# A fused attention and softplus MLP kernel: attention walked by batch in two windows, its instructions listed by a small planner, and a 512-token tail

## Chip, cores and metric

One core of a Trainium2 chip runs the whole program. The metric is the device time of one execution in microseconds, as the median of the runs taken. Five engines share the work: TensorE (PE, matmuls; PEld is its weight load), VectorE (DVE), ScalarE (ACT), GpSimd (POOL) and SyncE (SP, which here only issues DMAs).

## The reference

```python
# B, H, S, D = 4, 8, 576, 64; d_ff = 2048
scores = scale * q @ k.T          # causal mask, softmax over keys
local  = softmax(scores) @ v
q_p    = phi(q)                   # elu(q) + 1
mem    = (q_p @ M_prev) / (q_p @ z_prev + 1e-6)
out    = g * mem + (1 - g) * local          # g = sigmoid(beta), one per head
x      = out as [B * S, H * D]              # 2304 tokens x 512
y      = softplus(x @ w_in) @ w_out         # w_in, w_out arrive as 64-bit floats
```

Float32 accuracy is kept by splitting an operand into a rounded part and a remainder ("hi" and "lo") and adding three products (hi·hi, hi·lo, lo·hi). A product of the MLP is therefore three matmuls per 128-row slice.

## The kernel before

**Attention.** A unit is one batch and one pair of heads; 16 units run in the order batch, pair. Each has five chunks of query rows (four of 128, one of 64 rows for both heads). A chunk c goes: scores on PE (L292, mask L295), row maximum on DVE (L309), exponent on ACT (L312, written as a softplus with a shifted bias), reciprocal on DVE (L332, L333), the hi part on POOL (L337) and the lo part on DVE (L339), a DMA transpose from SP (L342), and two chunks later the product with the values on PE (L380, PSUM tile `xp`), where the memory term was put first (L369). ACT copies `xp` into the resident array `x` (L387). `prep_items` (L229) does a unit's value scaling and memory product; `loads` (L217) brings q, k and v for a unit.

**MLP.** The 16 f-tiles (128 of the 2048 columns) are handled in groups of 5, 5 and 6, since weights are decoded from 64-bit words on the chip (`split64`, L120: four DVE operations, two on POOL, one on ACT for each of two pieces of an f-tile). The tokens are cut into 8 blocks of 288 (`CAP`). For a block and an f-tile (an f-step here) there are 12 matmuls into `hp` (`emit_h`), a softplus and a split into `g` (`emit_g`), and 12 matmuls out. Group 0 of a block can run inside attention as a "fill" (`push_fill`, L180), once its whole batch has its `x`; the partial result goes to DRAM (`part`). The rest is phase 2 (L485 on): the blocks of group 0 that were not filled, then groups 1 and 2 over all 8 blocks. Each step splits its `x` block anew (`split_x`, L175; ACT and DVE in phase 2, DVE and POOL in a fill) and adds into `ps`, a resident sum; the last group stores each block. The output product of an f-step is issued three f-steps after its input product (`LAG`).

**What sets the order.** The framework's scheduler orders each engine's instructions by priority and a modelled time; every engine then runs its list strictly in that order. The number of fills in a slot is set by `credit` (L473), and weight pieces by `wcred` (L478).

Of the kernel before, what the change touches and what calls it, by code (L numbers as in the profile page):

```python
# [15 lines left out]
U32 = mybir.dt.uint32  # L16
# [8 lines left out]
TINY = 2.0 ** -15  # L25
# [4 lines left out]
GRPS = [5, 5, 6]  # L30
GA = GRPS[0]


class Unit:
    chunks = [0, 1, 2, 3, 4]

    def __init__(self, b, p):
        self.b, self.p = b, p
        self.pt = {}
        self.xp = None  # L40
# [3 lines left out]
def attn_softplus_moe(  # L44
# [13 lines left out]
    WIDE = w_in.dtype == I64  # L58

# [3 lines left out]

# [13 lines left out]
    wt = {}  # L77

    wa = ctx.enter_context(tc.tile_pool(name="wa", bufs=1, reuse_waits="tile"))
    moe1 = ctx.enter_context(tc.tile_pool(name="moe1", bufs=1))  # L80
    CAP = S // 2
    NFILL = 6
    nb = NT // CAP
    done = set()

    V, A, P, SY = nc.vector, nc.scalar, nc.gpsimd, nc.sync
# [11 lines left out]


    def load_w(pool, f, stage, sb, tag=None):  # L100
        t = pool.tile([128, 2, 2, 512], F32R, tag=tag or f"w{f}", name=f"w{f}")
        wt[f] = t

        def piece(i):
            src = w_out[f * 128:(f + 1) * 128, :] if i else w_in[f]
            hi, lo = t[:, i, 0, :], t[:, i, 1, :]
            if not WIDE:
                s = stage.tile([128, 512], F32, tag="ws", name="ws", bufs=sb)
                SY.dma_start(out=s, in_=src)
                cast(A, hi, s)  # L110
                sub(P, lo, s, hi)
            else:
                s = stage.tile([128, 1024], F32, tag="ws", name="ws", bufs=sb)
                tu = stage.tile([128, 512], F32, tag="wu", name="wu", bufs=sb)
                SY.dma_start(out=s.bitcast(I32), in_=src.bitcast(I32))
                split64(s, tu, hi, lo)

        return [lambda: piece(0), lambda: piece(1)]

    def split64(s, tu, hi, lo):  # L120

        sw = s.rearrange("p (e t) -> p e t", t=2)
        si = s.bitcast(I32).rearrange("p (e t) -> p e t", t=2)
        ti = tu.bitcast(I32)
        V.tensor_scalar(out=ti, in0=si[:, :, 1], scalar1=1, scalar2=1, op0=ALU.logical_shift_left,  # L125
                        op1=ALU.logical_shift_right)
        P.tensor_scalar(out=tu, in0=tu, scalar1=3.0e38, scalar2=TINY, op0=ALU.min, op1=ALU.max)  # L127
        V.tensor_scalar(out=ti, in0=ti, scalar1=3, scalar2=0x3FFFFFFF, op0=ALU.logical_shift_left,  # L128
                        op1=ALU.bitwise_and)
        V.scalar_tensor_tensor(out=ti, in0=si[:, :, 1], scalar=-0x40000000, in1=ti, op0=ALU.bitwise_and,  # L130
                               op1=ALU.bitwise_or)
        V.scalar_tensor_tensor(out=ti, in0=si[:, :, 0], scalar=29, in1=ti, op0=ALU.logical_shift_right,  # L132
                               op1=ALU.bitwise_or)
        cast(A, hi, tu)
        sub(P, lo, tu, hi)


    def mm3(out, pairs, start, stop):
        n = len(pairs)
        for i, (l, r) in enumerate(pairs):  # L140
            nc.tensor.matmul(out, lhsT=l, rhs=r, start=start and i == 0, stop=stop and i == n - 1)  # L141

    hcnt = []
    PB_ = {'h': 2, 'xp': 1, 'sm': 1}

    def emit_h(pool, f, xh, n, cap):
        w = wt[f]
        tags = ["h"] if not hcnt else ["h", "h", "xp", "sm"]
        tag = tags[hcnt[0] % len(tags)] if hcnt else "h"
        hp = ps_r.tile([128, 512], F32, tag=tag, name="hp", bufs=PB_[tag])  # L150
        if hcnt:
            hcnt[0] += 1
        pairs = []
        for kd in range(4):
            wh, wl = w[:, 0, 0, kd * 128:(kd + 1) * 128], w[:, 0, 1, kd * 128:(kd + 1) * 128]
            pairs += [(wh, xh[:, 0, kd, :n]), (wh, xh[:, 1, kd, :n]), (wl, xh[:, 0, kd, :n])]
        mm3(hp[:, :n], pairs, True, True)
        return hp

    def emit_g(pool, hp, n, cap, gb):  # L160
        l = pool.tile([128, cap], F32, tag="l", name="l", bufs=3)[:, :n]
        g = pool.tile([128, 2, cap], F32R, tag="g", name="g", bufs=gb)
        A.activation(out=l, in_=hp[:, :n], func=AF.Softplus)  # L163
        cast(A, g[:, 0, :n], l)
        sub(V if hcnt else P, g[:, 1, :n], l, g[:, 0, :n])
        return g

    def out_pairs(f, g, dm, n):
        w = wt[f]
        wh, wl = w[:, 1, 0, dm * 128:(dm + 1) * 128], w[:, 1, 1, dm * 128:(dm + 1) * 128]  # L170
        return [(wh, g[:, 0, :n]), (wh, g[:, 1, :n]), (wl, g[:, 0, :n])]

    fill = deque()

    def split_x(pool, t0, kd, xt, ea, eb):  # L175
        src = x[:, kd, t0:t0 + CAP]
        cast(ea, xt[:, 0, kd, :], src)
        sub(eb, xt[:, 1, kd, :], src, xt[:, 0, kd, :])

    def push_fill(k):  # L180
        st = {}
        t0 = k * CAP

        def xs(kd):
            if kd == 0:
                done.add(k)
                st["x"] = moe1.tile([128, 2, 4, CAP], F32R, tag="xhl", name="xhl", bufs=1)
            split_x(moe1, t0, kd, st["x"], V, P)

        def h(f):  # L190
            hp = emit_h(moe1, f, st["x"], CAP, CAP)
            st[f] = emit_g(moe1, hp, CAP, CAP, GA)

        def o(dm):
            op = ps_r.tile([128, 512], F32, tag="h", name="op", bufs=2)
            pairs = []
            for f in range(GA):
                pairs += out_pairs(f, st[f], dm, CAP)
            mm3(op[:, :CAP], pairs, True, True)
            pb = moe1.tile([128, CAP], F32, tag="pb", name="pb", bufs=2)  # L200
            A.copy(pb, op[:, :CAP])
            SY.dma_start(out=part[:, dm, t0:t0 + CAP], in_=pb)

        for kd in range(4):
            fill.append((0.0, kd == 0, lambda kd=kd: xs(kd)))
        for f in range(GA):
            fill.append((12 * CAP / 2400.0, False, lambda f=f: h(f)))
        for dm in range(4):
            fill.append((3 * GA * CAP / 2400.0, False, lambda dm=dm: o(dm)))


    units = [Unit(b, p) for b in range(B) for p in range(NP)]

    attn_ctx = ExitStack()
    at = attn_ctx.enter_context(tc.tile_pool(name="attn", bufs=1, side="right"))

    def loads(i):  # L217
        u = units[i]
        b, p = u.b, u.p
        u.kp = at.tile([128, S], F32, tag="kp", name="kp", bufs=2)  # L220
        u.va = at.tile([128, 640], F32, tag="va", name="va", bufs=2)
        u.mq = at.tile([128, 130 + S], F32, tag="mq", name="mq", bufs=2)
        SY.dma_start(out=u.mq, in_=nat[b, p, :, 640:770 + S])
        SY.dma_start(out=u.kp, in_=nat[b, p, :, 770 + S:])
        SY.dma_start(out=u.va, in_=nat[b, p, :, 0:640])
        u.vst = u.va.rearrange("p (c e) -> p c e", e=128)
        u.mz, u.qp = u.mq[:, 0:130], u.mq[:, 130:130 + S]

    def prep_items(i):  # L229
        u = units[i]  # L230
        p = u.p

        def v0():
            u.sc = at.tile([128, 5], F32, tag="sc", name="sc", bufs=3)
            si = u.sc.bitcast(I32)
            u.vb = at.tile([128, 2, 5, 128], F16, tag="vb", name="vb", bufs=2)
            jk = u.vb[:, 0].bitcast(BF16)
            for j, sg in enumerate((1.0, -1.0)):
                A.activation(out=jk, in_=u.vst, func=AF.Relu, scale=sg, accum_out=u.sc[:, 3 + j:4 + j])
            sp = ps_r.tile([128, 512], F32, tag="sm", name="sp", bufs=1)  # L240
            for j in range(2):
                nc.tensor.matmul(sp[:, 0:1], lhsT=mean, rhs=u.sc[:, 3 + j:4 + j], start=j == 0, stop=j == 1)
            V.tensor_scalar(out=si[:, 0:1], in0=sp.bitcast(I32)[:, 0:1], scalar1=0x7F800000, scalar2=None,
                            op0=ALU.bitwise_and)
            V.tensor_scalar(out=u.sc[:, 0:1], in0=u.sc[:, 0:1], scalar1=2.0 ** -60, scalar2=None, op0=ALU.max)
            V.tensor_scalar(out=si[:, 1:2], in0=si[:, 0:1], scalar1=-1.0, scalar2=float(261 << 23), op0=ALU.mult,
                            op1=ALU.add)
            V.tensor_scalar(out=u.sc[:, 2:3], in0=u.sc[:, 0:1], scalar1=2.0 ** -22, scalar2=None, op0=ALU.mult)
# [378 lines left out]
```

## Time and profile before

| | |
|---|---|
| median of 3 runs | 694.08 us (693.69 to 699.11) |
| profiled execution: span, first to last instruction | 695.3 us |
| mean granted TensorE clock | 0.937 of full speed |
| PE / DVE / ACT / POOL busy, share of span | 92% / 63% / 48% / 31% |
| HBM read, written | 34.89 MB, 7.08 MB |

The profile page gives no other time of that execution than its span. Busy shares are an average over a stage with attention, to about 353 us, and a stage with the MLP alone. A busy PE in the first stage isn't PE at its peak, since the ends of matmuls are modelled.

### The profile page before, as it was taken

What the parts mean: (1) busy time and instruction counts of PE and PEld (TensorE: products, weight loads), DVE (VectorE), ACT (ScalarE), POOL (GpSimd) and SP (SyncE); (2) the same over time, 40 slices, a digit from 0 to 9 for tenths busy, and PEclk for the clock granted to TensorE, in tenths of its full rate; (3) what the DMA queues carried; (4) which work ended last, traced back from release to release, by engine and by line L of the source; (5) the groups of instructions that cost most, each with busy time, mean ns of one, the idle gap of its engine ahead of it and who ended that gap; (6) DMA issues with size and microseconds to landing.
All of it is one profiled execution on the core that took longest, in us unless ns stands there. A gap on an engine that the chain in (4) does not pass through costs nothing.

```text
span 695.3 us, 12560 instructions
## 1 busy us (share of the span) xinstructions
PE 639.1 (92%) x4584; PEld 541.5 (78%) x4584; DVE 441.4 (63%) x1012; ACT 334.4 (48%) x949; POOL 219.0 (31%) x270
## 2 busy tenths in 40 slices
PE   6578976899999999997799999999999999999997
PEld 4344544667767666754689999999999999999997
DVE  4887999868776977858658799983333333323222
ACT  6554655457677556765354544353333333333321
POOL 3554565744544636324214545430000000000000
PEclk8667776899999999998899999999999999999999
DMA  4685778558676696747473333300000011110001
GB/s 151 154 195 131 156 170 180 95 112 185 126 150 136 111 171 128 160 107 131 80 225 110 122 119 102 115 31 1 1 1 1 1 35 35 35 35 25 28 29 59
DMA packets 124173, 68.47 MB, mean 98 GB/s; under 512 B 105680, under 2 KB 113872, under 8 KB 124112
## 3 DMA queue, kind: packets, MB, share of 16 engines
q1 hardware_dynamic: 124112, 67.67, 41.5%
q8 instruction: 36, 0.59, 0.4%
q14 instruction: 25, 0.20, 0.1%
HBM read 34.89 MB, written 7.08 MB: 60 GB/s over the span
## 4 chain that ended last, share of the span: by engine, by line
PE 37%; DVE 9%; DMA 3%; ACT 2%; issue 1%; POOL 1%; SPq 0%; DVEq 0%; ACTq 0%; POOLq 0%
PE acc L141 18%; PE hp L141 18%; DMA ws<-in_w_out_dram 2%; DVE wu L132 2%; DVE xhl L89 1%; DVE wu L130 1%; DVE wu L128 1%; DVE g L89 1%; DVE wu L125 1%; DVE PHL L339 1%; ACT P L312 1%; DVE ps L566 0%; DMA ws<-in_w_in_dram 0%; DMA PTB<-PHL 0%; ACT xhl L95 0%
## 5 line engine op out<-in xcount | busy, mean ns | idle before, releaser
L141 PE MATMUL hp<-xhl,w 128*128 128x288 f32 x1536 | 231.7, 300 | 5.7 <-DVE xhl L93 4.9
L141 PEld LDWEIGHTS hp<-xhl,w 128*128 128x128 f32 x1536 | 213.4, 191 | 8.0 <-DVE xhl L93 5.3
L141 PE MATMUL acc<-g,w 128*128 128x288 f32 x1296 | 188.6, 297 | 5.5 <-ACT P L312 2.9
L141 PEld LDWEIGHTS acc<-g,w 128*128 128x128 f32 x1296 | 177.8, 189 | 7.5 <-ACT P L312 3.0
L89 DVE TENSOR_TENSOR g<-l,g 128x288 fp32r<-128x288 f32 x108 | 57.9, 539 | 116.0 <-ACT g L95 116.0
L163 ACT ACTIVATE l<-hp 128x288 f32<-128x288 f32 x128 | 52.2, 411 | 139.2 <-PE hp L141 137.1
L337 POOL TENSOR_SCALAR PHL<-P,rr 128x128 f16<-128x128 f32 (+3 forms) x128 | 73.4, 587 | 107.6 <-DVE rr L333 22.2
L339 DVE SCALAR_TENSOR_TENSOR PHL<-P,rr,PHL 128x128 f16<-128x128 f32 (+3 forms) x128 | 89.6, 721 | 15.2 <-POOL PHL L337 14.0
L292 PE MATMUL s<-kp,mq 64*128 64x128 f32 (+3 forms) x256 | 67.8, 567 | 13.0 <-ACT P L312 11.3
L312 ACT ACTIVATE P<-s,nm 128x128 f32<-128x128 f32 (+3 forms) x128 | 66.2, 523 | 1.9
L95 ACT CAST g<-l 128x288 fp32r<-128x288 f32 x128 | 55.4, 435 | 20.5 <-PE acc L141 18.3
L380 PEld LDWEIGHTS <-vb 128*64 128x64 f16 x640 | 37.3, 118 | 31.2 <-issue 22.8
L89 POOL TENSOR_TENSOR w<-wu,w 128x512 fp32r<-128x512 f32 x32 | 47.7, 1493 | 32.5 <-ACT w L95 32.5
L309 DVE TENSOR_REDUCE nm<-s 128x2 f32<-128x256 f32 (+1 forms) x64 | 51.8, 813 | 7.1 <-PE s L295 7.1
L380 PE MATMUL xp<-PTB,vb 128*64 128x320 f16 (+2 forms) x448 | 43.5, 290 | 7.2 <-DMA PTB<-PHL 6.9
L566 DVE TENSOR_TENSOR ps<-acc,ps 128x288 f32<-128x288 f32 x64 | 27.4, 456 | 35.2 <-PE acc L141 35.2
L310 ACT ACTIVATE nm<-nm 128x2 f32<-128x2 f32 x64 | 12.8, 202 | 75.7 <-DVE nm L309 75.5
L89 DVE TENSOR_TENSOR xhl<-x,xhl 128x288 fp32r<-128x288 f32 x80 | 37.1, 515 | 17.4 <-ACT xhl L95 17.4
L95 ACT CAST w<-wu 128x512 fp32r<-128x512 f32 x32 | 19.9, 621 | 53.3 <-DVE wu L132 53.3
L292 PEld LDWEIGHTS s<-kp,mq 64*128 64x128 f32 x256 | 25.2, 221 | 23.6 <-ACT P L312 13.3
L127 POOL TENSOR_SCALAR wu<-wu 128x512 f32<-128x512 f32 x32 | 26.1, 817 | 54.3 <-DVE wu L125 44.8
L141 PE MATMUL op<-g,w 128*128 128x288 f32 x240 | 42.2, 311 | 0.0
(78 smaller groups left out, 714.6 us busy)
## 6 DMA issues: line engine op xcount, KB each, us to landing
ws<-in_w_in_dram SPq DMA_DIRECT2D x16, 512.0 KB, 3.4
ws<-in_w_out_dram SPq DMA_DIRECT2D x16, 512.0 KB, 3.6
mq<-in_nat_dram SPq DMA_DIRECT2D x16, 353.0 KB, 3.8
va<-in_nat_dram SPq DMA_DIRECT2D x16, 320.0 KB, 3.5
kp<-in_nat_dram SPq DMA_DIRECT2D x16, 288.0 KB, 3.9
out_dram<-ps SPq DMA_DIRECT2D x32, 144.0 KB, 1.8
part<-pb SPq DMA_DIRECT2D x16, 144.0 KB, 2.8
ps<-part SPq DMA_DIRECT2D x4, 576.0 KB, 8.0
```

Source lines behind the costliest of these rows:

```text
L89: eng.tensor_tensor(out=out, in0=in0, in1=in1, op=ALU.subtract)
L95: A.copy(out, in_)
L127: P.tensor_scalar(out=tu, in0=tu, scalar1=3.0e38, scalar2=TINY, op0=ALU.min, op1=ALU.max)
L141: nc.tensor.matmul(out, lhsT=l, rhs=r, start=start and i == 0, stop=stop and i == n - 1)
L163: A.activation(out=l, in_=hp[:, :n], func=AF.Softplus)
L292: nc.tensor.matmul(s[:, h, :n], lhsT=u.qp[r, c * 128:(c + 1) * 128], rhs=u.kp[r, :n], start=True, stop=True)
L309: V.tensor_reduce(out=nm, in_=s[:, :, :n], op=ALU.max, axis=AX.X, negate=True)
L312: A.activation(out=pt[:, h * n:h * n + n], in_=s[:, h, :n], func=AF.Softplus, scale=SCALE, bias=nm[:, h:h + 1], accum_out=l[:, h:h + 1])
L337: P.tensor_scalar(out=o[:, :, 0, h, :], in0=src, scalar1=r[:, h:h + 1], scalar2=0.0, op0=ALU.mult, op1=ALU.add)
L339: V.scalar_tensor_tensor(out=o[:, :, 1, h, :], in0=src, scalar=r[:, h:h + 1], in1=o[:, :, 0, h, :], op0=ALU.mult, op1=ALU.subtract)
L380: nc.tensor.matmul(u.xp[64 * h:64 * h + 64, lo:n], lhsT=u.vb[:, vi, kc, 64 * h:64 * h + 64], rhs=pt[:, kc * 4 + t * 2 + h, lo:n], start=False,
L566: V.tensor_tensor(out=o, in0=a, in1=o, op=ALU.add)
```

## The change

The diff rewrites nearly the whole body.

- **Order of attention:** for each batch, first window A (chunks 0 and 1, 256 tokens) of all four pairs, then window B (chunks 2, 3 and 4, 320 tokens) of all four pairs. Each window loads its own part of q and k, so k is loaded as 256 and later as 576 columns.
- **Blocks:** a block of the MLP is one window of one batch, 256 or 320 tokens, and can be filled when that window of the four pairs is done. Six of the eight blocks (`NFILL`) are filled, with six f-tiles each (`GA`) where it was five.
- **x:** no resident `x`. ACT writes the hi part and DVE the lo part straight from `xp`; a block's pair goes to DRAM (`xd`) and is loaded again for each step of phase 2.
- **Small operations:** three tiny DVE operations of the value scale go to POOL, and the normalisation of the memory term takes one DVE operation less in a window. In a fill, the lo part of `g` moves from POOL to DVE.
- **Order of engines:** every attention, decode and fill operation is declared with an engine, a duration, a rank and what it reads and writes. `Plan.run` lists them: at each point, the engine with the earliest start takes, among what can start within 60 ns, the lowest rank. The list is emitted as it is for all engines, SP too.
- **Phase 2:** two steps for the two blocks that were not filled (256 and 320 tokens, six f-tiles), then five steps of 512, 512, 512, 512 and 256 tokens with the other ten f-tiles in one group. The 20 weight pieces of these ten are decoded over the first 18 f-steps; while any is left, the lo part of `g` is made on POOL, later on DVE. The earlier partial sum is loaded for each step, added and stored.

```diff
-GRPS = [5, 5, 6]
-GA = GRPS[0]
+GA = 6
+CAP = 320
+WIDE_N = 512
+WINS = {"A": ([0, 1], 0, 256), "B": ([2, 3, 4], 256, 320)}
...
+            for e, lst in cand.items():
...
+                    s = max(free[e], o.ready, a)
+                    if e == "POOL":
+                        s = max(s, port["DVE"])
+                    elif o.port:
+                        s = max(s, port["POOL"])
...
+                s, _, o = min(((s, o.rank, o) for s, o in av if s <= m + 60.0), key=lambda v: v[1])
...
-    x = res.tile([128, NP, NT], F32, name="x")
...
+    xd = dram.tile([128, 2, 4, NT], F32, name="xd")
...
+    blocks = [(b * S + q0, n) for b in range(B) for _, q0, n in WINS.values()]
+    NFILL = len(blocks) - 2
...
+        op("ACT", 210 + .84 * n, k, lambda: A.activation(out=xh()[:, 0, p, :n], in_=xp()[:, :n], func=AF.Copy,
+                                                         scale=u.sc()[:, 2:3]), r=[xp, (u.sc, 1)], w=[(xh, p)])
+        op("DVE", 150 + 1.04 * n, k, lambda: V.scalar_tensor_tensor(
+            out=xh()[:, 1, p, :n], in0=xp()[:, :n], scalar=u.sc()[:, 2:3], in1=xh()[:, 0, p, :n], op0=ALU.mult,
+            op1=ALU.subtract), r=[xp, (u.sc, 1), (xh, p)], w=[(xh, 4 + p)])
...
+        op("SP", 700, k, lambda: SY.dma_start(out=xd[:, :, :, t0:t0 + n], in_=xh().bitcast(F32)[:, :, :, :n]),
+           r=[(xh, j) for j in range(8)], lat=2500)
+        if bi >= NFILL:
+            return
...
+    order = plan.run()
+    with tc.manual_schedule(engines=None):
+        for o in order:
+            o.fn()
+    attn_ctx.close()
...
+    steps = [(0, t0, n, range(GA)) for t0, n in blocks[NFILL:]]
+    t0 = 0
+    while t0 < NT:
+        n = min(WIDE_N, NT - t0)
+        steps.append((1, t0, n, range(GA, NF)))
+        t0 += n
...
+    nsw = sum(len(st[3]) for st in steps if not st[0]) + NF - GA - 4
...
+        xh[s] = moe2.tile([128, 2, 4, WIDE_N], F32R, tag="xhl", name="xhl", bufs=2)
+        for t in range(2):
+            SY.dma_start(out=xh[s].bitcast(F32)[:, t, :, :n], in_=xd[:, t, :, t0:t0 + n])
...
+            sub(P if dq else V, gs[i][:, 1, :n], l, gs[i][:, 0, :n])
+            while dq and (nd - len(dq)) * nsw < nd * (i + 1):
+                dq.popleft()()
```

## Rows read from the trace of the kernel before

**Rows 1.** Windows: stretch, its length, each engine's busy us (instructions), granted clock, DMA share, GB/s.

```profile
0.00:352.00 352.00, 302.33 (x2059) 206.92 (x2061) 272.24 (x678) 206.50 (x622) 166.75 (x226) 0.88 0.66 141
60.00:100.00 40.00, 33.90 (x192) 20.98 (x193) 34.57 (x85) 21.81 (x66) 21.22 (x26) 0.70 0.73 168
100.00:140.00 40.00, 30.50 (x177) 20.65 (x175) 35.96 (x76) 20.49 (x59) 25.45 (x31) 0.79 0.65 132
220.00:260.00 40.00, 38.51 (x294) 27.93 (x293) 32.35 (x78) 24.61 (x78) 19.51 (x27) 1.00 0.76 146
463.00:695.30 232.30, 228.77 (x1724) 228.30 (x1723) 72.89 (x172) 73.93 (x187) 0.95 (x1) 1.00 0.06 21
```

**Rows 2.** Costliest groups of the page, PE: matmuls of the MLP (busy us, mean ns).

```profile
L141 PE MATMUL hp<-xhl,w 128*128 128x288 f32 x1536 | 231.7, 300 | 5.7 <-DVE xhl L93 4.9
L141 PE MATMUL acc<-g,w 128*128 128x288 f32 x1296 | 188.6, 297 | 5.5 <-ACT P L312 2.9
L141 PE MATMUL op<-g,w 128*128 128x288 f32 x240 | 42.2, 311 | 0.0
```

**Rows 3.** Chain that ended last, in order of time: start us, us, what.

```profile
350.64 1.71 PE xp L380 x25
...
352.95 7.46 PE hp L141 x54
...
644.63 4.72 PE acc L141 x36
...
663.68 4.76 PE acc L141 x36
```

**Rows 4.** Timeline around the end of attention and of the span: start us, us, engine, line.

```profile
346.41 2.52 SPq L358 DMA_TRANSPOSE PTB<-PHL  x2
...
352.37 0.53 ACT L387 ACTIVATE x<-xp,sc 128x320 f32<-128x320 f32 x1 [6.39 <-PE xp L380]
...
690.86 1.07 PE L141 MATMUL acc<-g,w 128*128 128x288 f32 x6
```

**Rows 5.** Groups by line: DVE operations removed, moved or added like (L130: 40 to 352 us).

```profile
L89 DVE TENSOR_TENSOR g<-l,g 128x288 fp32r<-128x288 f32 x108 | 57.9, 539 | 116.0 <-ACT g L95 116.0
L566 DVE TENSOR_TENSOR ps<-acc,ps 128x288 f32<-128x288 f32 x64 | 27.4, 456 | 35.2 <-PE acc L141 35.2
L93 DVE CAST xhl<-x 128x288 fp32r<-128x288 f32 x16 | 7.0, 471 | 0.8 <-PE hp L141 0.8
L268 DVE TENSOR_SCALAR a<-np 128x6 f32<-128x6 f32 (+1 forms) x32 | 4.9, 152 | 1.6 <-PE np L267 1.6
L246 DVE TENSOR_SCALAR sc<-sc 128x1 int32<-128x1 int32 x16 | 2.4, 151 | 0.4
L130 DVE SCALAR_TENSOR_TENSOR wu<-ws,wu 128x512 int32<-128x512 int32 x8 | 5.8, 721 | 0.1
```

**Rows 6.** The same by line, from 350 to 460 us, where weights are decoded beside the MLP.

```profile
L89 POOL TENSOR_TENSOR w<-wu,w 128x512 fp32r<-128x512 f32 x21 | 31.3, 1496 | 22.3 <-ACT w L95 22.3
L127 POOL TENSOR_SCALAR wu<-wu 128x512 f32<-128x512 f32 x22 | 19.8, 899 | 41.4 <-DVE wu L125 41.4
L130 DVE SCALAR_TENSOR_TENSOR wu<-ws,wu 128x512 int32<-128x512 int32 x21 | 17.6, 840 | 0.3
```

**Rows 7.** Groups by line on POOL in the whole span.

```profile
L89 POOL TENSOR_TENSOR g<-l,g 128x288 fp32r<-128x288 f32 x20 | 19.0, 954 | 7.0 <-DVE rr L333 6.1 <-ACT g L95 0.8
L89 POOL TENSOR_TENSOR xhl<-x,xhl 128x288 fp32r<-128x288 f32 x16 | 14.2, 901 | 4.3 <-DVE xhl L93 4.3
```

**Rows 8.** DMA issues (KB each, median us to landing) and one wait (us in total, times, longest).

```profile
PTB<-PHL SPq DMA_TRANSPOSE x64, 3.6
ps<-part SPq DMA_DIRECT2D x4, 576.0 KB, 8.0
ws<-in_w_in_dram SPq DMA_DIRECT2D x16, 512.0 KB, 3.4
PE xp L380 <- DMA PTB<-PHL: 6.9, 10, 2.3
```

More of the change, by code (lines that the diff above doesn't have):

```diff
@@ new lines, with __init__, __call__ @@
+class Handle:
+    def __init__(self, ring, idx):
+        self.ring, self.idx = ring, idx
+        self.users, self.left, self.freed, self.open, self.t = [], 0, 0.0, False, None
+        self.w, self.rd = {}, {}
+    def __call__(self):
+        if self.t is None:
+            g = self.ring
+            self.t = g.pool.tile(g.shape, g.dtype, tag=g.tag, name=g.tag, bufs=g.bufs)
+        return self.t
+class Op:
+    __slots__ = ("eng", "dur", "fn", "rank", "lat", "port", "preds", "succs", "tiles", "n", "ready", "start", "end")
@@ new lines, with __init__, op, norm @@
+class Plan:
+    LAT = {"PE": 250.0, "DVE": 90.0, "ACT": 90.0, "POOL": 110.0, "SP": 0.0}
+    def __init__(self):
+        self.ops = []
+    def op(self, eng, dur, rank, fn, r=(), w=(), lat=0.0, port=False):
+        o = Op()
+        o.eng, o.dur, o.fn, o.rank, o.lat, o.port = eng, dur, fn, rank, lat, port
+        o.preds, o.succs, o.tiles = set(), [], []
+        def norm(items):
+            return [i if isinstance(i, tuple) else (i, 0) for i in items]
+        for h, k in norm(r):
+            o.preds.update(h.w.get(k, ()))
+            h.rd.setdefault(k, []).append(o)
+            o.tiles.append(h)
+        for h, k in norm(w):
+            o.preds.update(h.rd.pop(k, ()))
+            o.preds.update(h.w.get(k, ()))
+            h.w[k] = [o]
+            o.tiles.append(h)
+        o.preds.discard(o)
+        o.tiles = list(dict.fromkeys(o.tiles))
+        for h in o.tiles:
+            if h.ring is not None:
+                h.users.append(o)
+        self.ops.append(o)
+        return o
+    def run(self):
+        for o in self.ops:
+            o.n, o.ready = len(o.preds), 0.0
+            for q in o.preds:
+                q.succs.append(o)
+            for h in o.tiles:
+                h.left = len(h.users)
+        free = dict.fromkeys(self.LAT, 0.0)
+        port = {"DVE": 0.0, "POOL": 0.0}
+        cand = {e: [o for o in self.ops if o.eng == e and not o.n] for e in self.LAT}
+        order = []
+        def opens(o):
+            t = 0.0
+            for h in o.tiles:
+                if h.ring is None or h.open:
+                    continue
+                tl, i = h.ring.tiles, h.idx
+                if i and not tl[i - 1].open and tl[i - 1] not in o.tiles:
+                    return None
+                if i >= h.ring.bufs:
+                    old = tl[i - h.ring.bufs]
+                    if old.left:
+                        return None
+                    t = max(t, old.freed)
+            return t
+        while len(order) < len(self.ops):
+            best = None
+            for e, lst in cand.items():
+                av = []
+                for o in lst:
+                    a = opens(o)
+                    if a is None:
+                        continue
+                    s = max(free[e], o.ready, a)
[3 more added lines that the diff above has]
+                        s = max(s, port["POOL"])
+                    av.append((s, o))
+                if not av:
+                    continue
+                m = min(s for s, _ in av)
+                s, _, o = min(((s, o.rank, o) for s, o in av if s <= m + 60.0), key=lambda v: v[1])
+                if best is None or s < best[0]:
+                    best = (s, o)
+            s, o = best
+            o.start, o.end = s, s + o.dur
+            cand[o.eng].remove(o)
+            free[o.eng] = o.end
+            if o.eng == "POOL":
+                port["POOL"] = o.end
+            elif o.port:
+                port["DVE"] = o.end
+            for h in o.tiles:
+                if h.ring is not None:
+                    h.open = True
+                    h.left -= 1
+                    h.freed = max(h.freed, o.end + self.LAT[o.eng] + o.lat)
+            order.append(o)
+            for q in o.succs:
+                q.n -= 1
+                q.ready = max(q.ready, o.end + o.lat + (0.0 if q.eng == o.eng else self.LAT[o.eng]))
+                if not q.n:
+                    cand[q.eng].append(q)
+        self.order = order
+        return order
@@ L58, in attn_softplus_moe @@
     WIDE = w_in.dtype == I64
+    V, A, P, SY = nc.vector, nc.scalar, nc.gpsimd, nc.sync
+    MM = nc.tensor.matmul
     res = ctx.enter_context(tc.tile_pool(name="res", bufs=1))
@@ L120, in split64 @@
[L120 to L135, printed above, removed]
@@ L138, in mm3 @@
-    def mm3(out, pairs, start, stop):
-        n = len(pairs)
-        for i, (l, r) in enumerate(pairs):
[L141 to L209, printed above, removed]
@@ L212, in attn_softplus_moe @@
[L212 to L227, printed above, removed]
@@ new lines, in wpart, with in_pairs, out_pairs, mms @@
+    def wpart(f, i, t):
+        return wt[f][:, i, t, :]
+    def in_pairs(f, xh, kd, n):
+        wh, wl = (wt[f][:, 0, t, kd * 128:(kd + 1) * 128] for t in range(2))
+        return [(wh, xh[:, 0, kd, :n]), (wh, xh[:, 1, kd, :n]), (wl, xh[:, 0, kd, :n])]
+    def out_pairs(f, g, dm, n):
+        wh, wl = (wt[f][:, 1, t, dm * 128:(dm + 1) * 128] for t in range(2))
+        return [(wh, g[:, 0, :n]), (wh, g[:, 1, :n]), (wl, g[:, 0, :n])]
+    def mms(out, pairs, start, stop):
+        for i, (l, r) in enumerate(pairs):
+            MM(out, lhsT=l, rhs=r, start=start and i == 0, stop=stop and i == len(pairs) - 1)
@@ new lines, in v_prep, with acc, mn, ex @@
+    def v_prep(u, p, k):
+        va, vb, sc = u.va, u.vb, u.sc
+        def acc(j):
+            A.activation(out=vb()[:, 0].bitcast(BF16), in_=va(), func=AF.Relu, scale=1.0 - 2.0 * j,
+                         accum_out=sc()[:, 3 + j:4 + j])
+        for j in range(2):
+            op("ACT", 920, k, lambda j=j: acc(j), r=[va], w=[(vb, 0), (sc, 3 + j)])
+        sp = R["sm"].new()
+        def mn():
+            for j in range(2):
+                MM(sp()[:, 0, 0:1], lhsT=mean, rhs=sc()[:, 3 + j:4 + j], start=j == 0, stop=j == 1)
+        op("PE", 250, k, mn, r=[(sc, 3), (sc, 4)], w=[sp])
+        def ex():
+            V.tensor_scalar(out=sc().bitcast(I32)[:, 0:1], in0=sp().bitcast(I32)[:, 0, 0:1], scalar1=0x7F800000,
+                            scalar2=None, op0=ALU.bitwise_and)
+        def scale():
+            si = sc().bitcast(I32)
+            P.tensor_scalar(out=sc()[:, 0:1], in0=sc()[:, 0:1], scalar1=2.0 ** -60, scalar2=3.0e38, op0=ALU.max,
+                            op1=ALU.min)
+            P.tensor_scalar(out=si[:, 1:2], in0=si[:, 0:1], scalar1=-1.0, scalar2=float(261 << 23), op0=ALU.mult,
+                            op1=ALU.add)
+            P.tensor_scalar(out=sc()[:, 2:3], in0=sc()[:, 0:1], scalar1=2.0 ** -22, scalar2=0.0, op0=ALU.mult,
+                            op1=ALU.add)
+            P.tensor_scalar(out=sc()[:, 5:7], in0=g15[:, 2 * p:2 * p + 2], scalar1=sc()[:, 0:1],
+                            scalar2=2.0 ** -7, op0=ALU.mult, op1=ALU.mult)
+        op("DVE", 150, k, ex, r=[sp], w=[(sc, 0)])
+        op("POOL", 450, k, scale, r=[(sc, 0)], w=[(sc, 1)])
+        op("ACT", 830, k + .6, lambda: A.activation(out=vb()[:, 0], in_=va(), func=AF.Copy, scale=sc()[:, 1:2]),
+           r=[va, (sc, 1)], w=[(vb, 0)])
+        op("DVE", 880, k + 1.3, lambda: V.scalar_tensor_tensor(
+            out=vb()[:, 1], in0=va(), scalar=sc()[:, 1:2], in1=vb()[:, 0], op0=ALU.mult, op1=ALU.subtract),
+           r=[va, (sc, 1), (vb, 0)], w=[(vb, 1)], port=True)
@@ new lines, in attn_softplus_moe @@
+    A.preload_act_table_set("softplus")
+    SY.dma_start(out=bsb, in_=beta.unsqueeze(0).to_broadcast([128, H]))
+    consts()
+    warm = ps_r.tile([128, 512], F32, tag="h", name="warm", bufs=2)
+    with tc.high_priority(offset=-100000):
+        for _ in range(40):
+            MM(warm[:, :128], lhsT=identb, rhs=identb, start=True, stop=True)
+    order = plan.run()
[3 more added lines that the diff above has]
+    attn_ctx.close()
+    wb = ctx.enter_context(tc.tile_pool(name="wb", bufs=1, side="right", reuse_waits="tile"))
@@ new lines, in attn_softplus_moe, with next_x @@
+    for f in range(GA, NF):
+        for i in range(2):
+            dq.append(lambda f=f, i=i: load_w(f, i))
+    nd = len(dq)
+    nsw = sum(len(st[3]) for st in steps if not st[0]) + NF - GA - 4
+    seq = [(s, f) for s, st in enumerate(steps) for f in st[3]]
+    LAG = 3
+    xh, gs, acc, pp = {}, {}, {}, {}
+    def next_x(s):
+        _, t0, n, _ = steps[s]
+        xh[s] = moe2.tile([128, 2, 4, WIDE_N], F32R, tag="xhl", name="xhl", bufs=2)
+        for t in range(2):
+            SY.dma_start(out=xh[s].bitcast(F32)[:, t, :, :n], in_=xd[:, t, :, t0:t0 + n])
@@ new lines, in attn_softplus_moe @@
+    HT = [("h", 2), ("h", 2), ("xp", 1), ("sm", 1)]
+    next_x(0)
+    for i in range(len(seq) + LAG):
+        if i < len(seq):
+            s, f = seq[i]
+            g_, t0, n, fl = steps[s]
+            if f == fl[0] and s + 1 < len(steps):
+                next_x(s + 1)
+            tag, bufs = HT[i % 4]
+            hp = ps_r.tile([128, 512], F32, tag=tag, name="hp", bufs=bufs)
+            for kd in range(4):
+                mms(hp[:, :n], in_pairs(f, xh[s], kd, n), kd == 0, kd == 3)
+            l = moe2.tile([128, WIDE_N], F32, tag="l", name="l", bufs=3)[:, :n]
+            gs[i] = moe2.tile([128, 2, WIDE_N], F32R, tag="g", name="g", bufs=LAG + 2)
+            A.activation(out=l, in_=hp[:, :n], func=AF.Softplus)
+            cast(A, gs[i][:, 0, :n], l)
+            sub(P if dq else V, gs[i][:, 1, :n], l, gs[i][:, 0, :n])
+            while dq and (nd - len(dq)) * nsw < nd * (i + 1):
+                dq.popleft()()
+        j = i - LAG
+        if j < 0:
+            continue
+        s, f = seq[j]
+        g_, t0, n, fl = steps[s]
+        first, last = f == fl[0], f == fl[-1]
+        if first:
+            acc[s] = [ps_s.tile([128, 2, 512], F32, tag="s", name="acc") for _ in range(2)]
+            if g_:
+                pp[s] = moe2.tile([128, 4, WIDE_N], F32, tag="pp", name="pp", bufs=2)
+                SY.dma_start(out=pp[s][:, :, :n], in_=part[:, :, t0:t0 + n])
+        g = gs.pop(j)
+        for dm in range(4):
+            a = acc[s][dm // 2][:, dm % 2, :n]
+            mms(a, out_pairs(f, g, dm, n), first, last)
+            if last and g_:
+                o = pp[s][:, dm, :n]
+                V.tensor_tensor(out=o, in0=a, in1=o, op=ALU.add)
+                SY.dma_start(out=outT[dm * 128:(dm + 1) * 128, t0:t0 + n], in_=o)
+            elif last:
+                o = moe2.tile([128, CAP], F32, tag="pb", name="pb", bufs=2)[:, :n]
+                A.copy(o, a)
+                SY.dma_start(out=part[:, dm, t0:t0 + n], in_=o)
```

650 lines of the change are left out of this document (318 added, 332 removed).

## Prediction

> **What bounds the kernel now.** I read the windows first, to part the span into stages. To 352 us there is attention with some fills; from there PE is busy nearly without a break, 228.8 of 232.3 us after 463 us at the full granted clock, 1.00, the 2.4 GHz level [rows 1]. So the second stage is bound by PE. Its unit price comes from the chain: the last output product of a six-f-tile step starts at 644.63 and that of the next step at 663.68 us [rows 3]. That is 19.05 us for 6 x 24 = 144 matmuls, 132.3 ns each. At 2.4 GHz 288 columns take 120.0 ns, so 12.3 ns of each matmul don't stream columns.
>
> A check of this price: phase 2 holds 1296 `acc` matmuls [rows 2] and as many into `hp`, 2592. At most some 36 of them stand ahead of the hand-over, by my reading of the timeline; 2556 x 0.1323 is 338 us, and from 352.95 [rows 3] to the end of the last matmul at 691.93 us [rows 4] it is 339. Phase 2 holds no idle time worth a gain.
>
> The first stage is not bound by PE. It takes 352 us for 16 units, 22.0 us each, and its pace is much the same where there are no fills and the clock is 0.70 as where there are fills and it is 1.00. What stands out in each window is DVE: 34.6 of 40 us from 60 to 100, 36.0 from 100 to 140 us, 32.4 in the middle, 272.2 of 352 in all (77%) [rows 1]. ACT has 59% and POOL 47% there. DVE with its waits sets the pace, and PE has room that fills could use. The reader is to see two stages with different prices: a matmul in phase 2 costs 132 ns of the end, a matmul put into attention costs little as long as DVE is what is late.
>
> **Moving matmuls into attention.** Fills now hold 20 f-steps: the 240 `op` matmuls [rows 2] are four blocks by five f-tiles by 12. The change fills 6 x 6 = 36. The 16 f-steps that leave phase 2 are 384 matmuls, 50.8 us at 132.3 ns. Inside attention they add 50.8 us of PE work. I cost it at nothing there, and the cover is DVE: 480 fill matmuls now and 864 then are 63.5 and 114.3 us, beside attention's own PE work. In the middle of attention, 220 to 260 us, the fills already run at about the density that 864 in 325 us would need, with the pace of a unit unchanged. If that cover fails, up to 50.8 us come back.
>
> **The length of attention.** I take it from DVE's work. Removed: 16 casts of x, 7.0 us; 32 operations of the memory normalisation, 4.9 us; and three scalar operations a unit that go to POOL, 48 at about 0.15, 7.1 us [rows 5]. Added: the lo part of `g` for 36 f-steps at 0.539, 19.4 us; the lo part of x from PSUM, 32 at 0.456 by the nearest row with a PSUM operand, 14.6 us; two more weight pieces, 2 x 2.4 us (two operations of 0.72 [rows 5], and about 0.9 in the other two) = 4.7 us. The sum is 272.2 - 19.0 + 38.7 = 291.9 us. POOL gets lighter: 19.0 us of `g` and 14.2 us of x leave it [rows 7], some 14 us come. ACT gains the fixed parts of shorter operations and 16 more f-steps, some 30 us on 206; it stays under DVE. SP gets more loads, but it computes nothing.
>
> How full DVE will be is not in the trace. One end is today's mean, 0.773: 291.9 / 0.773 = 378 us. The other is 0.97: 301 us. I take 0.90, the fullest window of today [rows 1], since blocks now come free by half batches and the first fill no longer waits for a whole batch: 324 us.
>
> **Phase 2.** First 12 f-steps of 256 and 320 tokens, 288 matmuls at 132.3 on average: 38.1 us. Then four steps of 512 tokens, 4 x 240 matmuls, and one of 256, 240 matmuls. A 512-column matmul is not in the trace. If the 12.3 ns are fixed, it takes 213.3 + 12.3 = 225.6 ns; if they vanish, 213.3; if they grow with the columns, 235.2. I take the fixed one, as the rest looks like a change of weights, which comes once for a matmul: 960 x 0.2256 = 216.6 us (ends 204.8 and 225.8). For 256 columns it gives 119.0 ns, 28.6 us. In all 283.3 us, where 2592 of today's matmuls would be 342.9.
>
> What would the Trainium skill make of this? Its page TensorE: Matmul & The Clock Gate (section Back-to-back issue gap) spaces matmuls at the high clock by the columns over 2.4 plus about 2.5 ns. For 288 columns that is 122.5 ns, and the rows show 132.3, so the trace does not agree with it here; for 512 columns it would be 215.8 ns and the sum would be 9 us less.
>
> **Decoding beside it.** Within the first 12 f-steps (38.1 us of PE) 13 of the 20 pieces are decoded. On POOL a piece is 1.496 + 0.899 = 2.40 us in that company [rows 6], 31 us for 13, and now 12 lo parts of `g` at 0.954 [rows 7], 11 us, lie on the same queue: 42.6 us against 38.1. If the two longer DVE operations of a piece (0.840 each [rows 6]) also keep POOL waiting, it is 64 us; three f-steps of lag, 9.5 us, are slack. What waits behind POOL is `g`, and behind `g` the output products on PE's queue. Ends 0 and 17 us; I take 8, nearer the plain sum.
>
> **The hand-over.** Today PE goes on 0.6 us after the last attention product, at 352.95 [rows 3, 4]. Then x must be split by ACT and DVE (0.5 + 0.5), stored, and the first block of phase 2 loaded. That load stands behind the last store on SP's list, and about 2.4 MB are then in flight; a load of 512 KB lands after 3.4 us, and 576 KB pieces, four at once, after 8.0 [rows 8]. With issue that is 6 to 10 us of idle PE, or nothing where unfinished fills cover it. I take 8. The tail after the last matmul is today's 695.3 - 691.9 = 3.4 us.
>
> **The sum.** 324 + 8 + 283.3 + 8 + 3.4 = 626.7 us, against a span of 695.3. The median of the runs is 1.2 us below that span; so 626 us.
>
> **Rivals.**
>
> *Attention keeps today's fullness.* The list is fixed and each engine runs it strictly; durations that differ from the listed ones leave the same gaps as now. For it: even with a scheduler, DVE had 77%. Against it: windows at 86 to 90%. Time: 378 in place of 324, 679 us. Chance 0.17.
>
> *Attention grows until it eats the gain.* The place is PE's list, at the product that waits for a transposed tile. DMA engines are busy 0.76 of the time with transposes and loads already [rows 1], a transpose lands after 3.6 us, and that wait is only 6.9 us in all now [rows 8]. The change stores 9.4 MB of x in the same stage and reloads k, and a load or store that waits on SP's list holds the transposes behind it. If each unit once waits one more landing, 22.0 + 3.6 = 25.6 us, attention takes 410 us and the kernel 711 us. It decides from an attention of 392 us, 24.5 us a unit. Against it: k and x add about a fifth to the DMA work, at a share that still leaves room. Chance 0.10.
>
> *All of it works.* DVE at 0.97 (301 us), weight changes hidden under 512 columns (12 us less), no loss in decoding, a hand-over of 4 us: 579 us. Chance 0.12; the page's spacing above goes the same way.
>
> The forecast has the remaining 0.61.
>
> **How the numbers follow.** The range is 588 to 680: it reaches over the first rival and leaves out most of the last (about 0.1) and the second (0.10). A difference under 1% can't be told from none here. Faster by over 1% means below 687: the forecast, the last rival, and 0.14 of the first rival's 0.17, 0.87. Within 1%: 0.03 of the first and 0.01 of the second, 0.04. Slower: the second, 0.09.
>
> **What would show it.** In the changed trace the first MLP-only matmul after attention should stand near 332 us, and DVE should be near 36 of 40 us in most windows before. 240 matmuls of 512 columns should take 54 us at a granted clock of 1.00; 51 or 56 would decide about the 12 ns. `g` waiting for POOL, and PE for `g`, should show some 8 us in the first 50 us of phase 2, and PE an idle gap of about 8 us at the hand-over. The prediction is wrong if attention ends after 392 us; PE's wait for `PTB` would then be far over 6.9 us. It is wrong in kind if attention is shorter but PE, not DVE, is what is full there.

## The result and the profile after

The changed kernel takes 670.39 us (median of 4 runs, 666.93 to 673.6) against 695.56 us in the same session: a ratio of 0.963, 95% interval 0.958 to 0.968. I had forecast 626 us: the direction is right and the time lies in the range, but the gain is 25 us where I said 68. The profiled execution of the changed kernel has a span of 671.8 us.

The chain of the changed kernel around the hand-over and in phase 2 (start us, us, what):

```profile
362.94 6.10 DMA xd<-xhl
369.49 5.20 DMA xhl<-xd
374.73 6.78 PE hp L277 x44
381.51 1.44 PE acc L277 x12
...
388.71 1.76 PE hp L277 x12
...
512.12 2.80 PE acc L277 x12
...
657.28 1.36 PE acc L277 x12
```

Its timeline: the last x of the first batch, PE's first product of phase 2 after 11.53 us of idle time, and the last six matmuls.

```profile
124.76 0.53 ACT L568 ACTIVATE xhl<-xp,sc 128x320 fp32r<-128x320 f32 x1 [2.41 <-PE xp L562]
...
373.29 1.20 PE L277 MATMUL hp<-xhl,w 128*128 128x256 f32 x4 [11.53 <-DMA xhl<-xd]
...
667.65 0.97 PE L277 MATMUL acc<-g,w 128*128 128x256 f32 x6 [0.18 <-DVE pp L736]
```

The last x (ACT's copy out of `xp` for the last window) is read at 361.8 us, when the last attention product ends; by this time I compare the experiments. Against my sum of 626.7 us for this span:

| term | forecast | measured | difference |
|---|---|---|---|
| end of attention's products | 324 | 361.8 | +37.8 |
| hand-over to steady PE, 374.73 | 8 | 12.9 | +4.9 |
| phase 2 to the end of the last matmul, 668.62 | 291.3 | 293.9 | +2.6 |
| tail | 3.4 | 3.2 | -0.2 |

So 38 of the 45 us are the length of attention. Windows of the changed kernel (columns as in [rows 1]): all of attention, and its steady part.

```profile
0.00:362.00 362.00, 307.24 (x2376) 237.63 (x2376) 269.69 (x652) 232.40 (x705) 158.49 (x274) 0.92 0.80 174
125.00:310.00 185.00, 169.34 (x1372) 135.48 (x1372) 133.98 (x337) 128.41 (x394) 71.43 (x137) 0.97 0.83 174
```

And the kernel before in the same steady part, not shown ahead of the prediction:

```profile
125.00:310.00 185.00, 177.96 (x1312) 128.48 (x1311) 140.00 (x353) 117.87 (x360) 90.07 (x119) 0.99 0.67 135
```

and its mark of the first batch:

```profile
113.30 0.51 ACT L387 ACTIVATE x<-xp,sc 128x320 f32<-128x320 f32 x1
```

DVE, which I had said would be 90% full, is 72% full in the steady part (134.0 of 185) and 75% over all of attention. What went up is the share of the DMA engines, 0.67 to 0.83. From the last x of the first batch to the last of all, before takes 352.4 - 113.3 = 239.1 us for 12 units, after 361.8 - 124.8 = 237.0: 19.9 and 19.8 us a unit. The steady pace has not changed, though 36 f-steps are filled where it was 20. The first batch got 11.5 us later; spreading its decoding (below) gave back 8 us of that, and they were lost again in the last two batches.

### The profile page after: what moved, and what is told of

It is laid out like the page before. It is cut to its first block, busy times and chain, and to the rows that moved or that the text cites. A ratio compares the mean times of both kernels' runs of the same rounds, so it can differ in the third digit from the quotient of the medians.

```text
span 671.8 us, 10879 instructions
## 1 busy us (share of the span) xinstructions
PE 599.8 (89%) x3864; PEld 484.6 (72%) x3864; DVE 375.8 (56%) x797; ACT 311.8 (46%) x857; POOL 219.8 (33%) x332
## 3 DMA queue, kind: packets, MB, share of 16 engines
q1 hardware_dynamic: 147840, 96.79, 57.3%
## 4 chain that ended last, share of the span: by engine, by line
PE 62%; DMA 15%; DVE 13%; ACT 4%; issue 3%; POOL 1%; SPq 1%; DVEq 0%; ACTq 0%; POOLq 0%
PE hp L277 18%; PE acc L277 17%; PE h L277 12%; PE xp L562 6%; DMA PTB<-PHL 5%; PE s L370 4%; DMA PTA<-PHL 4%; DMA ws<-in_w_in_dram 3%; DVE PHL L423 3%; DVE wu L257 2%; PE sm L526 2%; DVE wu L253 1%; PE s L377 1%; DVE wu L249 1%; PE xp L550 1%
## 5 line engine op out<-in xcount | busy, mean ns | idle before, releaser
L277 PE MATMUL hp<-xhl,w 128*128 128x512 f32 (+2 forms) x744 | 156.4, 360 | 14.1 <-DMA xhl<-xd 11.8
L277 PE MATMUL acc<-g,w 128*128 128x512 f32 (+2 forms) x744 | 154.1, 356 | 0.2 <-DVE pp L736 0.2
L277 PEld LDWEIGHTS hp<-xhl,w 128*128 128x128 f32 x744 | 125.4, 191 | 37.3 <-issue 11.6
L277 PEld LDWEIGHTS acc<-g,w 128*128 128x128 f32 x744 | 123.8, 188 | 22.4 <-DVE pp L736 0.4
L277 PE MATMUL h<-g,w 128*128 128x256 f32 (+1 forms) x432 | 70.8, 308 | 0.0
L277 PE MATMUL h<-xhl,w 128*128 128x256 f32 (+1 forms) x432 | 69.7, 313 | 0.0
L277 PEld LDWEIGHTS h<-xhl,w 128*128 128x128 f32 x432 | 62.0, 199 | 0.4
L277 PEld LDWEIGHTS h<-g,w 128*128 128x128 f32 x432 | 60.3, 192 | 1.2 <-ACT gl L592 0.2
L216 ACT CAST w<-wu 128x512 fp32r<-128x512 f32 x32 | 19.8, 617 | 61.6 <-DVE wu L257 61.6
L216 ACT CAST g<-l 128x512 fp32r<-128x512 f32 (+2 forms) x62 | 33.8, 551 | 22.0 <-PE acc L277 20.7
L370 PE MATMUL s<-kB,qB 64*128 64x384 f32 (+1 forms) x128 | 35.0, 623 | 9.5 <-ACT P L388 6.1
```

What stands on the lines that cost most here:

```text
L216: A.copy(out, in_)
L277: MM(out, lhsT=l, rhs=r, start=start and i == 0, stop=stop and i == len(pairs) - 1)
L370: MM(sv[:, h, :n], lhsT=qv[rr, cq:cq + 128], rhs=kv[rr, :n], start=True, stop=True)
```

## The experiments

Each undoes or relieves one thing in the changed kernel; its "last x" stands for the end of attention, read from one profiled execution. The changed kernel and two versions below have the same list of instructions in attention, and their last x stand at 361.8, 360.4 and 357.3 us: differences of some 5 us mean nothing. `PTA` and `PTB` are the transposed softmax tiles of the windows A and B. The lines that give the last x (timeline, ACT) follow for seven kernels: one third of the fills' products; x stored twice from SP; the lo part of g on POOL; half of the transposes; x stored twice, from ACT; half of the transposes and one third of the products; x kept, four staging buffers.

```profile
359.54 0.53 ACT L568 ACTIVATE xhl<-xp,sc 128x320 fp32r<-128x320 f32 x1 [5.78 <-PE xp L562]
```

```profile
382.14 0.53 ACT L569 ACTIVATE xhl<-xp,sc 128x320 fp32r<-128x320 f32 x1 [1.28 <-PE xp L563]
```

```profile
358.39 0.53 ACT L568 ACTIVATE xhl<-xp,sc 128x320 fp32r<-128x320 f32 x1 [4.12 <-PE xp L562]
```

```profile
334.95 0.53 ACT L569 ACTIVATE xhl<-xp,sc 128x320 fp32r<-128x320 f32 x1 [1.19 <-PE xp L563]
```

```profile
375.59 0.53 ACT L569 ACTIVATE xhl<-xp,sc 128x320 fp32r<-128x320 f32 x1 [1.81 <-PE xp L563]
```

```profile
317.89 0.53 ACT L569 ACTIVATE xhl<-xp,sc 128x320 fp32r<-128x320 f32 x1 [2.37 <-PE xp L563]
```

```profile
357.33 0.53 ACT L569 ACTIVATE xhl<-xp,sc 128x320 fp32r<-128x320 f32 x1 [1.19 <-PE xp L563]
```

**PE relieved.**

```diff
-mms(hp()[:, :n], in_pairs(f, xh(), kd, n), kd == 0, kd == 3)
+mms(hp()[:, :n], in_pairs(f, xh(), kd, n)[:1], kd == 0, kd == 3)   # the same for out_pairs
```

> The fills inside attention issue one of the three products (288 of 864 matmuls; the hi-hi one), every other operation stays: it leaves out two thirds of the first six f-tiles' products for six blocks. 576 matmuls of 119 to 146 ns are 76 us less on PE. In the changed kernel the last x is read out of PSUM at 361.8 us. Theory PE (from 100 us on PE's list sets the pace, fills included): it falls to 325 us or below. Theory DVE (DVE with its waits sets the pace, as I predicted): 350 to 365 us. Theory DMA (the DMA engines, full while window A runs, set it): 350 to 365 us.

Last x at 359.5 us, 2 us earlier, which is no difference; the time was 675.63 us in one run. Its attention in one window, to compare with the first window above:

```profile
0.00:362.00 362.00, 267.86 (x1800) 178.85 (x1800) 273.65 (x653) 230.46 (x705) 158.93 (x274) 0.81 0.78 174
```

The 576 matmuls are gone (1800 for 2376), but PE's busy time fell by 39 us and not by 76: the mean granted clock of this stretch fell from 0.92 to 0.81, so the matmuls that are left ran longer. Even so, 39 us less of PE moved nothing, and theory PE falls, although PE led the chain from 125 to 310 us of the changed kernel (110 of 186 us). A chain says what PE did while other things were late. PE's wait for `PTB` rose from 14.0 to 27.6 us: the products came to the transposed tiles sooner and waited there.

**More to store, on SP's queue and on ACT's; DVE relieved.**

```diff
+op("SP", 700, k, lambda: SY.dma_start(out=xd2[...], in_=xh()...), r=[(xh, j) for j in range(8)], lat=2500)
```

> Each block's x is stored a second time, into another DRAM tensor: 9.4 MB more written in attention, some 27 us of all sixteen DMA engines at the 350 GB/s that a share of 0.06 at 21 GB/s stands for. Theory DMA: the last x is read 15 us later or more (over 376 us). Theories PE and DVE: within 5 us of 361.8 us.

```diff
+op("ACT", 100, k, lambda: A.dma_start(out=xd2[...], in_=xh()...), r=[(xh, j) for j in range(8)], lat=2500)
```

> The second store of each x block again, now issued from ACT's queue and not from SP's. If the 20 us of the doubled store were time of the DMA engines, the last x is read at 376 to 384 us again. If they were the store's place on SP's list ahead of the transposes, it stays at 359 to 366 us.

```diff
-op("DVE", 150 + 1.04 * n, -1, lambda: sub(V, g lo ...), port=True)
+op("POOL", 200 + 2.1 * n, -1, lambda: sub(P, g lo ...), port=True)
```

> In the fills the lo part of g is made on POOL instead of DVE, 36 operations: 17.4 us less on DVE, about 30 us more on POOL. Theory DVE: the last x is read 15 to 23 us earlier (about 342 us). Theories PE and DMA: within 5 us of 361.8 us, or later, where fills wait for POOL.

From SP the doubled store moves the last x to 382.1 us, 20 us later; from ACT to 375.6, 14 us later, just under the band I gave. So most of it is not the place on SP's list. (The times were 699.98 and 693.83 us, 673.37 for the third, in one run each.) The third gives 358.4 us, no difference either. But it did not test theory DVE as I had meant it to:

```profile
0.00:362.00 362.00, 309.53 (x2376) 237.16 (x2376) 267.26 (x617) 234.30 (x705) 186.06 (x310) 0.91 0.80 175
```

The 36 operations, 17.5 us, have left DVE, and its busy time is only 2.4 us less (267.3 for 269.7): its other operations took some 15 us longer beside 28 us more of work on POOL. What settles theory DVE is the next experiment.

**Half of the transposes, alone and with PE relieved.**

```diff
-o = phl()[...].rearrange("p (k t h s) -> p k t h s", t=2, h=2, s=128)
+o = phl()[...].rearrange("p (t k h s) -> p k t h s", t=2, h=2, s=128)
-out=ptw()[:, 0:4 * nk, ...], in_=phl()[:, 0:nk * 512]
+out=ptw()[:, 0:2 * nk, ...], in_=phl()[:, 0:nk * 256]
...                                             # the same for the chunk of 64 rows
-rhs=ptw()[:, kc * 4 + t * 2 + h, lo:n]
+rhs=ptw()[:, kc * 2 + h, lo:n]
```

> Only the hi parts of the softmax tiles are transposed (the lo parts are still made, but not moved; the product that used them takes the hi part again, so the lo part of the softmax is left out of the output). That is half of the transposed bytes, some 12.5 of 25.7 MB; every matmul and every vector operation stays. After the first runs (PE relieved by 76 us: last x at 359.5; DVE by 17 us: 358.4; 9.4 MB more stored: 382.1; the changed kernel: 361.8 us) theory DMA is that the transfers, transposes above all, set the pace of attention: the last x is then read at 340 us or earlier. Rival: the order of the list and its waits do, and 9.4 MB of stores only came in the way on SP's list: 352 to 362 us.

> Half of the transposes and one third of the fills' products at once (the lo part of the softmax and two thirds of the fills' products are left out). With half the transposes alone the last x was read at 335.0 us, and PE showed 53 of 53 us busy from 235 to 288 us. If PE is what is next when the transfers are relieved, the last x falls to 315 us or below; if DVE and its waits are, it stays at 328 to 336 us.

Last x at 335.0 us, 27 us earlier, with every matmul and vector operation still there (2376 and 652 up to that point, as in the changed kernel) and the same list; the time was 650.85 us in one run, and 631.16 for the second kernel. Windows of the first kernel up to its last x and in the steady part, and of the second in the steady part:

```profile
0.00:335.50 335.50, 300.46 (x2376) 230.45 (x2376) 271.13 (x652) 233.35 (x705) 158.58 (x274) 0.92 0.61 150
125.00:310.00 185.00, 182.60 (x1510) 144.30 (x1511) 152.06 (x376) 142.70 (x435) 81.27 (x147) 0.99 0.65 152
```

```profile
125.00:310.00 185.00, 155.65 (x1191) 103.05 (x1191) 164.09 (x406) 148.03 (x463) 86.72 (x154) 0.95 0.66 156
```

DVE has the same work, 271.1 us, in 27 us less, so its work was not the bound; theory DVE, on which my forecast rested, falls. The DMA share falls to 0.65 and PE and DVE do more in the same 185 us. The chain over 125 to 310 us held 30.4 us of transposes in the changed kernel and 5.0 us here. How heavy the transposes are shows in the DMA queues of the pages: the half left out is 12.6 MB in 49,152 packets and 84 us of all sixteen engines (57.3% of 671.8 us against 46.3% of 649.1), where the 9.4 MB of the second store from ACT are 8,320 packets and 30 us. Then PE counts: with two thirds of the fills' products gone as well, the last x is at 317.9 us, 17 us earlier, where without the relief of the transposes the same cut gave 2. That is 3 us above the band for "PE is next" and 10 under the one for DVE; I read it as PE first, with others close behind, which is not shown. DVE is 89% full there (164.1 of 185), the first time near my 0.90.

**Weights spread out.** `DEC0, DECS = 1.0, 1.15` becomes `1.0, 2.3`.

> The twelve weight pieces of attention are spread over 26 slots of 80 and not over 14. The first batch took to 124.8 us and each later one 77 to 82 us; with the last x of the first batch as the mark: if DVE's 27 us of decoding at the front hold the first batch, it ends 8 to 15 us earlier (110 to 117 us) and attention 5 to 12 us earlier, unless the fills, which then start later, pile up at the end. If start-up is held by transfers and the first loads, the mark moves by less than 4 us.

The first batch's last x came at 116.8 us in place of 124.8, as expected, and that of the second at 195.5 in place of 206.8, but that of attention at 363.7 (361.8). So the gain was lost in the last two batches, where nothing is decoded any more. What had moved there are fills, as I had feared: some 570 of their 864 matmuls start after 207 us, and some 495 in the changed kernel. The time was 676.98 us in one run.

**The hand-over.**

```diff
+xpool = ctx.enter_context(tc.tile_pool(name="xpool", bufs=1))   # ring xhl, 512 wide, lives on
-next_x(0)
+for s in range(2):
+    xh[s] = xhs[NFILL + s]()
```

> The two last blocks' x stay in on-chip memory for the first two steps of phase 2 (the ring of x lies outside the attention pool and is 512 wide), instead of being loaded back from DRAM. The gap between the last attention product and the first product of phase 2 was 361.77 to 373.29 us. Theory: the gap is that round trip, it falls to 3 us or less and the time by 9 to 12 us, to about 659 us, ratio to the kernel before 0.947. Rival: something else holds the first steps too (freed memory, the decoding of weights), the gap goes to the first waits for g or w and the time falls by less than 4 us.

The gap closed (PE was busy 38.0 of 38 us from 362 to 400 us), but the time stayed: 670.97 us, ratio 0.963 (0.960 to 0.967). The 11.5 us came back as waits for weights. Windows of this kernel, and below them those of the next, with four staging buffers:

```profile
362.00:400.00 38.00, 38.00 (x269) 36.91 (x268) 14.11 (x20) 14.67 (x35) 21.01 (x23) 1.00 0.83 298
400.00:450.00 50.00, 40.72 (x161) 30.61 (x160) 34.37 (x45) 14.89 (x27) 28.41 (x26) 0.93 0.36 119
```

```profile
362.00:400.00 38.00, 38.00 (x260) 36.55 (x259) 25.41 (x27) 14.40 (x34) 25.09 (x26) 1.00 0.86 309
400.00:450.00 50.00, 47.29 (x202) 36.68 (x201) 42.53 (x51) 15.87 (x28) 35.77 (x29) 1.00 0.36 122
```

```diff
-s = wb.tile([128, 1024], F32, tag="ws", name="ws", bufs=2)
+s = wb.tile([128, 1024], F32, tag="ws", name="ws", bufs=4)     # and pp: bufs=1
```

> As the kernel that keeps the last two blocks of x on chip, with four staging buffers for weights in phase 2 where there were two (and one buffer for the earlier partial sum where there were two). Keeping x closed the gap of 11.5 us, but PE then idled between 400 and 450 us, on weights: DVE waited 40 us for their loads. Theory: two staging buffers and a landing of some 4 us bound the decoding; with four the idle time goes and the time falls to about 660 us (8 to 12 us less than 671). Rival: the seven operations of a piece on DVE, POOL and ACT bound it; less than 4 us.

656.48 us, ratio 0.942 (0.939 to 0.946): 2% better than the change, and the best version I have. Of the 14 us that it gains over the one with two buffers, 3 lie in attention (last x at 357.3 for 360.4 us), where the two don't differ. DVE's waits for the weights' loads from 362 to 480 us fell from 40.1 us (23.8 and 16.3) to 12.8 (11.9 and 0.9), and its work in the 88 us of these windows rose from 48.5 to 67.9 us: the landing of a load with two buffers had bounded the decoding, and the gap before it had hidden that by giving decoding a head start.

**x stored once.** If transfers hold attention, writing less should shorten it. Three versions store x as float32 once, and split it again in phase 2.

```diff
+op("ACT", 210 + .84 * n, k, lambda: A.activation(out=xf()[:, p, :n], in_=xp()[:, :n], ...), r=[xp, ...], w=[(xf, p)])
-SY.dma_start(out=xd[:, :, :, t0:t0 + n], in_=xh()...)
+SY.dma_start(out=xd[:, :, t0:t0 + n], in_=xf()[:, :, :n])
```

> As the kernel with x kept and more staging buffers (three here), but a block of x is stored once, as float32, by one more ACT operation of about 0.5 us for each half unit, and split again in phase 2: 4.7 MB less written in attention, 4.7 MB less read in phase 2. By the doubled store (9.4 MB cost 14 and 20 us) theory DMA has the last x read 7 to 10 us earlier than the 357.3 us of the kernel it starts from, about 349 us, and a time of about 649 us (656.5 before). Rival: below today's traffic something else holds attention, or the extra ACT operations do; last x at 355 us or later, time 653 us or more.

> As the kernel that stores x once, with two buffers for that float32 x (one buffer less for g and for the partial sums of the fills makes the room). There the windows B got about 3 us shorter than in the kernel it started from, and the windows A 5 to 8 us longer. If the single buffer did that (a block's first x waits until the last block's store has landed), the A windows come back, the last x is read at about 346 us and the time is about 648 us. If the additional ACT operation on the list did it, A windows stay long: 360 us or later, 658 us or more.

> The two kernels that store x once read the float32 x out of the PSUM tile on ACT, and DVE then waited for that operation (30 us in all) and PE for the tile (15 us). Here POOL adds the hi and lo parts from on-chip memory instead, off that tile, with one float32 buffer. If the longer hold of the one PSUM tile made the windows A longer, they come back, and with 4.7 MB less to write the last x is read at 345 to 352 us and the time is 645 to 652 us. If 4.7 MB less in attention buy nothing, the last x stays at 357 us or later and the time at 655 us or more.

All three missed. The times are 662.74, 665.71 and 664.93 us (ratios 0.950, 0.953 and 0.952, no interval reaching that of the version without it), the last x at 366.5, 367.3 and 364.4 us. The single buffer alone was not the reason, nor the longer hold of `xp` alone: each was taken away in its turn, but the other stayed, so both together are not excluded. 4.7 MB less, bought with 32 more operations and another list, made attention 7 to 10 us longer. In the third version all of that lies in the first batch (its last x at 135.8 us, 125.2 without it); the twelve units after it took 228.6 us for 232.1, which is no difference.

## Why the prediction was wrong

**Moving matmuls into attention: right.** "I cost it at nothing there": the steady pace is the same, 19.8 against 19.9 us a unit, with 16 f-steps more, and taking two thirds of the fills' products out gives 2 us. But "the cover is DVE" was wrong; the cover is whatever makes the transposed tiles late. And "the pace of a unit unchanged" was a loose reading: the last three units of the kernel before, with hardly a fill and no decoding, took 16.6 us each (x at 302.7 and 352.4 us).

**The length of attention: the step that failed.** It said "I take it from DVE's work" and "I take 0.90". DVE's work was near: 269.7 us against 291.9 (its operations ran shorter; the 128 lo parts of the softmax take 632 ns in the mean, and 721 before). Its fullness was 0.745, where before had 0.773 and I had taken 0.90. I had taken the busiest engine in the windows for the bound. It was not: with the same work on it, attention ends 27 us earlier when half of the transposes are left out. Transfers were what relief and load both moved, 27 us earlier with half of the transposes, 14 to 20 us later with 9.4 MB more. I had these rows in hand, a DMA share of 0.66 to 0.76 [rows 1], and used them in the slower rival alone, where one landing more a unit was to be added to today's pace. What happened lies between: PE's wait for `PTB` doubled, from 6.9 to 14.0 us, the share went to 0.83, and the pace of a unit stayed. Over all of attention the DMA engines were busy for 290 us (0.80 of 362) where before had 232 (0.66 of 352), a quarter more and not the fifth that I had set against that rival. That the additional stores and loads ate what the list won is my reading; no run has the list without them. The first rival, "attention keeps today's fullness", gave 679 us and is the nearest, with its mechanism half right: the gaps stayed, and half of the transposes left out closes 27 us of them; that the durations in the list had no part in them is not shown.

**Phase 2: nearly right in sum, by two errors that mostly cancel.** A 512-column matmul takes 2.80 us / 12 = 233.3 ns, and not 225.6: the extra time grows with the columns (9.4%, where 288 columns had 10.3% [rows 3]), and the 240 take 56.0 us, my mark for that. 960 matmuls cost 224.0 us, 7.4 more. The spacing that the Trainium skill gives for a single matmul (TensorE: Matmul & The Clock Gate, Back-to-back issue gap), 215.8 ns for 512 columns, is further off than 225.6 or 235.2. The 240 matmuls of 256 columns in the last step take 27.2 us at 113.3 ns, 1.4 less. And PE is idle for 2.5 of the 293.9 us (busy 291.4 from 374.73 to 668.62), and not for 8. The rest, 40.2 us for the first 288 matmuls, is 2.1 more than I said; from 374.7 to 380 us the granted clock is 0.73.

**The hand-over: right in place, a little short.** The load stood behind the last store on SP, as said; 12.9 us against 8. But the block that it brings is the other one, window A of the last batch, which SP had sent to DRAM at 316 us: by the chain its load waited until the store of window B had landed, at 369.04 us, and why is open. What I had not seen is that it was hidden cost: closing it alone gave nothing until decoding had more buffers.

**What stays open.** Whether the transposes hold attention by the share of the DMA engines, by their landing in the chain (for `PTB`, median 4.0 us in the changed kernel, 3.0 with half of them) or by the time of SP's queue to issue them is not told apart: halving them changes all three. For the long transposes of `PTB` (L431) that time is 1.92 us in the median, and 1.23 with half of them; in the steady part SP issues for some 135 of the 185 us, and for some 100 in the kernel before. And why storing less did not help is open too; the list, the operations and the traffic changed together. The first two of these versions lowered the DMA share of the steady part from 0.84 to 0.77 and got no shorter, which speaks against the share alone.

## What to carry to other kernels

The fullest engine of a stage is not its bound until taking work from it moves the end; here taking work from PE moved nothing, and DVE did the same work in 27 us less once half of the transposes were gone. Look, too, at what a relief really relieves: 76 us of matmuls left out made PE's busy time 39 us shorter, and 17 us of operations moved off DVE made its busy time 2 us shorter. A busy PE on the chain can be filling time. Two costs in sequence can hide one another: closing an 11.5 us gap gained nothing until the next limit, two staging buffers, was lifted with it, and 14 us then (3 of them in attention).

## What the runs showed of the hardware

At the granted clock of 1.00 and with a weight load for each matmul, float32r matmuls came every 113 to 120 ns for 256 columns, 132 for 288, 147 for 320 and 233.3 for 512: near 2.2 columns a nanosecond at every width (2.13 to 2.26), so wide tiles saved almost nothing here. The same 9.4 MB of stores cost attention 20 us from SP's queue and 14 us from ACT's, in one run each. By time of the DMA engines a megabyte of these transposes weighed twice a megabyte of stores and more: 84 us for 12.6 MB against 30 us for 9.4 MB. And with fewer matmuls in attention PE was granted a lower mean clock there, 0.81 for 0.92.
